# Turning a recurrence's outputs into matmul features by VectorE block transposes and a trip through DRAM

## The chip, the cores and the metric

One core of a Trainium2 chip runs the program. The metric is the device time of one execution in microseconds (us). Before the change three runs gave 671.13, 673.59 and 679.51 us; the median is 673.59. The profile is one further execution, taken by the hardware profiler.

A core has five engines with a queue each, run in order: PE (TensorE, the matmuls), DVE (VectorE), ACT (ScalarE), POOL (GpSimd) and SP (SyncE, which here issues nearly all DMAs). They wait for one another by semaphores. Matmul results land in PSUM, from which DVE or ACT carry them to SBUF.

## The reference

The inputs are q, k and v (4 x 8 x 768 x 48: batch, head, token, width) and beta (4 x 8 x 768). Two blocks follow each other:

```python
k_n = k / (np.linalg.norm(k, axis=-1, keepdims=True) + 1e-06)
for t in range(S):                               # a recurrence per (batch, head)
    y[:, :, t] = q_t @ state
    v_old = k_t @ state
    state = state + b_t * outer(k_t, v_t - v_old)
x = y.transpose(0, 2, 1, 3).reshape(3072, 384)   # 4*768 tokens, 8 heads x 48
h = x @ w_in                                     # 384 -> 2048
out = (h * np.cos(h)) @ w_out                    # 2048 -> 384
```

## The kernel before

**Units and pairs.** The 768 tokens are cut into 24 units of 32 tokens. A unit n holds 32 tokens of all 4 batches and 8 heads; the partitions are 4 batches x 32 tokens. Inside a unit the recurrence becomes matrices: `gram(n)` (PE) multiplies keys with keys and queries; a triangular matrix per head is inverted column by column, for a pair of units at once, by POOL (`inverse`, lines L656 and L663; the first pair by DVE). The way to the inverse leads through DRAM: `gram_put` writes g_dr, `gram_get` reads it as gb, `put` writes z_dr, `get(n)` reads zt. Then per unit, on PE: `state(n)` (keys and queries times the state, into the PSUM tile p_kq), `solve(n)` (p_u, from zt and the right side rhs), `update(n)` (p_s, the state's increment), `within(n)` (adds the part from inside the unit to p_kq). DVE carries out what lies between (`right`, `solve_out`, `update_out`, which changes the state st that `state(n+1)` reads).

**Outputs to features.** After `within(n)` the outputs y lie in p_kq with tokens on partitions. The second block needs features on partitions. So `within_out(n)` (L825, ACT) copies p_kq to the SBUF tile y, `features(n)` (L829, PE) transposes y in three 128 x 128 steps into the PSUM tile p_z (which shares the single bank "two" with p_g, p_u and p_s), and `features_out(n)` (L839, ACT) copies p_z into one half of x_ffn, which holds the features of a pair p of units (2p and 2p+1).

**The second block** runs on pairs. For pairs 0 and 1 `hidden` (L856) multiplies x_ffn with w_in directly. From pair 2 on `x_sum(p)` (L927, DVE) forms differences of the features, one in place, and `layer(p, s, i)` (L975) uses a scheme of sums that needs fewer products. ACT and DVE compute h cos(h): `turns`, `rest`, `cos`, `gate`. `output` (L1001, pair 0) or `product` (L1058) multiply by w_out; `collect` sums; SP stores.

**Weights** arrive as 64-bit words: `weights` (SP), `split` (ACT), `shift` (DVE), `add` (POOL), 28 pieces in the first part of the run.

**The order.** The class `Order` keeps a list of tasks. Every task has a key, an engine, tiles that it makes and uses, and what it depends on. `LINE` is a list of 1,879 numbers written out in the file: the order in which the tasks' instructions are emitted. `run` (L157) follows it, and every engine's queue is pinned to it. So the sequence on each engine is fixed by LINE, and the costs given to `add` do not act at run time. Tiles rotate through few buffers: one p_kq, one "two", one y, two zt, two x_ffn.

## Time and profile before

| what | value |
|---|---|
| three runs | 671.13, 673.59, 679.51 us |
| span of the profiled execution | 670.2 us |
| DVE busy, whole span | 466.5 us, 70% |
| ACT | 242.4 us, 36% |
| POOL | 347.1 us, 52% |
| p_z transposes (L835) on PE | 72 of them, 273 ns median, 12.2 us busy |
| y copies (L827) and x_ffn copies (L843) on ACT | 24 each, 478 ns median |
| DVE transposes kq_t<-qp (L531), 128x1024 | 16, 1,236 ns median |
| DVE transpose t_beta<-bq (L376), 128x768 | 1, 968 ns |
| SP's DMA queue | 212,516 packets, 49.16 MB |

The span is the time from the first to the last recorded event of the core; the measured time of a run lies a little above it. "Busy" is the time in which an instruction of that engine was running; matmuls overlap, so their single durations add up to more than the time that they take from PE. "SPq" is the queue of SP, whose rows are the issue of DMAs and not the moving of the data. A row such as "L835 PE MATMUL p_z<-consts,y x3" names line, engine, operation, the tile written and the tiles read, and the count. In a list of waits a row has the waiting engine and group, the engine and group that released it, and then the us in total, the times, and the longest.

### The profile page before, as it was taken

Reading aid. Unit: us, or ns where it says so; the run is one execution under the profiler, and the core shown is the slowest. Engines: PE = TensorE matmul, PEld = TensorE weight load, DVE = VectorE, ACT = ScalarE, POOL = GpSimd, SP = SyncE. Lnnn points to the kernel's source line nnn. Section 1 sums busy time; section 2 is a strip of 40 time slices with the busy share of each in tenths; the row PEclk is TensorE's granted clock in tenths of the full one; section 3 lists DMA queues with packets and bytes.
Section 4 is the critical chain, followed back from the end, with each engine's and each line's share of the span. In section 5 each row is a group of like instructions: output and inputs, shape, how many; then the busy total and the mean of one; then the engine's idle time right before and its main releaser. Section 6 shows DMA issues by size and latency. Waiting matters only on the chain.

```text
span 670.2 us, 27723 instructions
## 1 busy us (share of the span) xinstructions
PE 616.5 (92%) x12120; PEld 580.5 (87%) x12120; DVE 466.5 (70%) x892; ACT 242.4 (36%) x416; POOL 347.1 (52%) x734
## 2 busy tenths in 40 slices
PE   4326789999999999999999999999999999999996
PEld 3225779976889999999999999999999999999996
DVE  6872698897577777787767767777776666656662
ACT  3441565650223433334334332333323333332420
POOL 4268778988728658238458484385383382000000
PEclk9999899999899999999999999999999999999999
DMA  8776594464364523544443624623312302000000
GB/s 179 183 177 156 130 228 124 105 110 66 53 103 68 85 54 57 89 88 70 70 83 55 108 35 73 106 39 53 69 27 39 68 2 40 20 2 24 1 25 24
DMA packets 215645, 51.80 MB, mean 77 GB/s; under 512 B 207076, under 2 KB 210420, under 8 KB 215524
## 3 DMA queue, kind: packets, MB, share of 16 engines
q1 hardware_dynamic: 212516, 49.16, 38.0%
q8 instruction: 95, 1.56, 1.0%
q10 hardware_dynamic: 2752, 0.43, 0.4%
q0 software_dynamic: 256, 0.44, 0.2%
q14 instruction: 26, 0.21, 0.1%
HBM read 39.24 MB, written 10.75 MB: 75 GB/s over the span
## 4 chain that ended last, share of the span: by engine, by line
PE 79%; DMA 7%; SPq 4%; POOL 4%; DVE 2%; issue 2%; ACT 0%; ACTq 0%; DVEq 0%; POOLq 0%
PE p_h L975 28%; PE p_out L1058 27%; PE p_h L856 5%; PE p_kq L713 4%; PE p_out L1001 3%; PE p_u L776 3%; PE p_s L799 3%; PE p_kq L816 2%; PE p_g L546 2%; POOL z L663 2%; DMA pairs<-in_moe_w_in_dram 2%; POOL part L656 2%; PE p_o L1058 2%; DMA qp<-in_q_dram 1%; SPq L310 1%
## 5 line engine op out<-in xcount | busy, mean ns | idle before, releaser
L656 POOL TENSOR_TENSOR part<-z,gb 128x126 f32<-128x126 f32 (+22 forms) x341 | 134.6, 395 | 116.1 <-DMA gb<-g_dr 75.0
L663 POOL TENSOR_TENSOR z<-z,part 128x126 f32<-128x126 f32 (+22 forms) x341 | 138.7, 407 | 26.7
L975 PE MATMUL p_h<-x_ffn,w_in 128*128 128x128 f32 x1120 | 143.0, 277 | 0.0
L975 PEld LDWEIGHTS p_h<-x_ffn,w_in 128*128 128x128 f32 x1120 | 134.2, 192 | 1.5
L1058 PE MATMUL p_out<-w_out,g_ffn 128*128 128x192 f32 x672 | 121.8, 330 | 2.0 <-issue 2.0
L1058 PEld LDWEIGHTS p_out<-w_out,g_ffn 128*128 128x128 f32 x672 | 108.7, 191 | 3.3 <-issue 2.1
L896 ACT ACTIVATE turns<-p_h,quarter_turn 128x512 int32<-128x512 f32 x96 | 65.8, 688 | 105.6 <-DVE p_h L994 72.1
L912 ACT ACTIVATE turns<-turns,halfpi 128x512 f32<-128x512 f32 x96 | 68.7, 721 | 64.3 <-DVE turns L903 63.7
L1058 PE MATMUL p_out<-w_sum,g_ffn 128*128 128x192 f32 x496 | 88.7, 329 | 0.0
L903 DVE SCALAR_TENSOR_TENSOR turns<-p_h,turns 128x512 f32<-128x512 f32 x96 | 65.3, 683 | 22.0 <-ACT turns L896 22.0
L1058 PEld LDWEIGHTS p_out<-w_sum,g_ffn 128*128 128x128 f32 x496 | 79.7, 190 | 0.8
L991 ACT COPY g_ffn<-p_h 128x512 f32<-128x512 f32 x60 | 35.0, 584 | 108.8 <-PE p_h L975 108.7
L1074 DVE TENSOR_TENSOR g_ffn<-g_ffn 128x512 f32<-128x512 f32 x88 | 62.3, 715 | 10.0 <-PE p_out L1058 8.9
L915 DVE TENSOR_TENSOR g_ffn<-turns,p_h 128x512 f32<-128x512 f32 x96 | 64.6, 677 | 6.6 <-ACT turns L912 6.5
L994 DVE TENSOR_TENSOR p_h<-g_ffn,p_h 128x512 f32<-128x512 f32 x60 | 41.5, 692 | 30.5 <-PE p_h L975 23.7
L467 POOL TENSOR_TENSOR knrm<-ksum,halves 128x16 f32<-128x16 f32 (+1 forms) x14 | 36.2, 2590 | 41.5 <-DVE ksum L455 41.5
L1108 DVE SCALAR_TENSOR_TENSOR o<-p_out,o 128x192 f32<-128x192 f32 x74 | 25.2, 353 | 35.4 <-PE p_out L1058 33.9
L856 PE MATMUL p_h<-x_ffn,w_in 128*128 128x128 f32 x384 | 47.3, 282 | 2.3 <-POOL part L656 2.1
L856 PEld LDWEIGHTS p_h<-x_ffn,w_in 128*128 128x128 f32 x384 | 45.8, 197 | 3.3 <-issue 2.2
L975 PE MATMUL p_h<-x_sum,in_sum 128*128 128x128 f32 x320 | 41.6, 277 | 0.0
L786 DVE TENSOR_TENSOR u<-p_u,bz 128x384 f32<-128x384 f32 x48 | 24.4, 550 | 21.9 <-PE p_u L776 21.8
L975 PEld LDWEIGHTS p_h<-x_sum,in_sum 128*128 128x128 f32 x320 | 38.7, 192 | 0.5
(110 smaller groups left out, 767.2 us busy)
## 6 DMA issues: line engine op xcount, KB each, us to landing
pairs<-in_moe_w_in_dram SPq DMA_DIRECT2D x12, 512.0 KB
pairs<-in_moe_w_out_dram SPq DMA_DIRECT2D x16, 384.0 KB
gb<-g_dr SPq DMA_DIRECT2D x22, 256.0 KB
vp<-in_v_dram SPq DMA_DIRECT2D x96, 48.0 KB
out_dram<-o SPq DMA_DIRECT2D x23, 192.0 KB
kp<-in_k_dram SPq DMA_DIRECT2D x128, 24.0 KB
z_dr<-z SPq DMA_DIRECT2D x11, 256.0 KB
zt<-z_dr SPq DMA_DIRECT2D x88, 32.0 KB
```

The source lines that it names most:

```text
L467: nc.gpsimd.tensor_tensor(out=scales[m][2][:, part], in0=sums[m, part.start][:, 0:n], in1=halves[:, 0:n], op=ALU.pow,)
L656: eng.tensor_tensor(out=part, in0=z[:, 0:rows, j, None].to_broadcast(shape), in1=a[:, j, None, j + 1 :].to_broadcast(shape), op=ALU.mult,)
L663: eng.tensor_tensor(out=behind, in0=behind, in1=part, op=ALU.subtract)
L856: nc.tensor.matmul(p_h[:, i], w_in[:, t, (4 * k + i) * 128 : (4 * k + i + 1) * 128], xts[p][:, t, unit * 128 : (unit + 1) * 128], start=(t ...
L896: nc.scalar.activation(turns[p, f], hidden_of(p, f), AF.Identity, bias=quarter_turn, scale=TURN)
L903: nc.vector.scalar_tensor_tensor(out=r, in0=hidden_of(p, f), scalar=TURN, in1=t, op0=ALU.mult, op1=ALU.subtract,)
L912: nc.scalar.activation(r, r, AF.Sin, bias=halfpi, scale=2.0 * math.pi)
L915: nc.vector.tensor_tensor(out=place(p, f), in0=step_of(rests.pop((p, f)), f), in1=step_of(hidden_of(p, f), f), op=ALU.mult,)
L975: nc.tensor.matmul(p_h[:, e], in_sum[:, odd_tile, 4 * s + e] if a == "s" else w_in[:, a, f * 128 : (f + 1) * 128], x_sums[p][:, unit] if b ...
L994: nc.vector.tensor_tensor(out=block(p, s, 0, 1) if i == 3 else p_h, in0=block(p, s, *one), in1=p_h, op=ALU.add,)
L1058: nc.tensor.matmul(p_o, left(p, part, a)[:, e % 4], right(e, b), start=(e == 0), stop=(e == FT // 2 - 1), skip_group_check=True,)
L1074: nc.vector.tensor_tensor(out=left(p, s, to), in0=left(p, s, one), in1=left(p, s, two), op=op)
```

## The change

For units 4 and later (`MOVED = 4`) the three steps from p_kq to x_ffn are replaced:

- `within_turn(n)` on DVE: one stream transpose of the 384 output columns of p_kq into the SBUF tile y. It turns each block of 32 tokens x 32 features in its place, so that y has 32 features on the 32 partitions of a batch.
- `within_put(n)` on SP: four DMAs, one a batch, write y to a DRAM tile y_dr laid out as 128 features x 4 batches x (3 x 32): pieces of 96 numbers, 384 bytes.
- `features_move(n)` on SP: one DMA reads y_dr into the half of x_ffn, 128 partitions of 384 numbers.

x_ffn changes its layout for all units, from [128, 3, 256] to [128, 2, 4, 3, 32]: unit, batch, feature block, token. What reads it (`hidden`, `layer`, `x_sum`) takes four runs of 32 columns in place of one run of 128. Units 0 to 3 keep the transposes on PE.

`LINE` is another order of the tasks throughout, from the first loads to the last unit. Two tasks at the start (the load of beta and its spreading) now also account for the buffers that they hold.

```diff
@@ constants
+    MOVED = 4
@@ after features(n)
     def features_out(n):
         if n % 2 == 0:
-            xts[n // 2] = ffn_pool.tile([128, KT, TOK], FP, name="x_ffn")
-        cols = slice((n % 2) * 128, (n % 2 + 1) * 128)
-        nc.scalar.copy(xts[n // 2][:, :, cols], p_zs.pop(n))
+            xts[n // 2] = ffn_pool.tile([128, 2, B, KT, C], FP, name="x_ffn")
+        nc.scalar.copy(
+            xts[n // 2][:, n % 2].rearrange("p b k t -> p k b t"),
+            p_zs.pop(n).rearrange("p k (b t) -> p k b t", t=C),
+        )
+
+    def moved(p, t, unit):
+        return xts[p][:, unit, :, t]
+
+    def within_turn(n):
+        y = ys[n] = work.tile([128, KT * 4, C], FP, name="y", bufs=1)
+        nc.vector.transpose(
+            y.rearrange("p (z k) t -> p k z t", k=KT),
+            p_kqs.pop(n)[:, :, 1].rearrange("p a j e -> p j a e"),
+        )
+
+    def within_put(n):
+        y = ys[n]
+        ys[n] = dram.tile([128, B, KT * C], FP, name="y_dr")
+        dst = ys[n].rearrange("(z i) b c -> b i z c", i=C)
+        for b in range(B):
+            nc.sync.dma_start(
+                out=dst[b], in_=y[quarter(b)].rearrange("i (z k) t -> i z (k t)", k=KT)
+            )
+
+    def features_move(n):
+        if n % 2 == 0:
+            xts[n // 2] = ffn_pool.tile([128, 2, B, KT, C], FP, name="x_ffn")
+        nc.sync.dma_start(
+            out=xts[n // 2][:, n % 2].rearrange("p b k t -> p b (k t)"), in_=ys.pop(n)
+        )
@@ hidden, layer: the moving operand
-                    xts[p][:, t, unit * 128 : (unit + 1) * 128],
+                    moved(p, t, unit),
@@ x_sum
-        t = x_sums[p] = ffn_pool.tile([128, 3, 128], FP, name="x_sum", bufs=1)
-        u0, u1 = slice(0, 128), slice(128, 256)
+        t = x_sums[p] = ffn_pool.tile([128, 3, B, C], FP, name="x_sum", bufs=1)
         for to, one, two in (
-            (t[:, 1], xt[:, 1, u1], xt[:, 0, u1]),
-            (xt[:, 0, u1], xt[:, 0, u1], xt[:, 0, u0]),
...
+            (t[:, 1], moved(p, 1, 1), moved(p, 0, 1)),
+            (moved(p, 0, 1), moved(p, 0, 1), moved(p, 0, 0)),
...
@@ the tasks of a unit, after within(n)
+        if n >= MOVED:
+            add(("within_turn", n), "DVE", 0.5, lambda: within_turn(n), [("within", n)],
+                makes=[("y", ("y", n))], uses=[("p_kq", n)])
+            add(("within_put", n), "SP", 0.45, lambda: within_put(n), [("within_turn", n)],
+                makes=[("y_dr", ("y_dr", n))], uses=[("y", n)], moves=1.0)
+            add(("features_out", n), "SP", 1.8, lambda: features_move(n),
+                [("within_put", n)] + ([("features_out", n - 1)] if second else []),
+                makes=[] if second else [("x", ("x", m))], uses=[("y_dr", n)], moves=1.0)
+            return
```

Around units 4 and 5 the two orders stand as follows on PE (keys of tasks; the number in parentheses is the unit, or pair and step):

```
before: solve(4) out(1,0,0) update(4) within(4) out(1,0,1) features(4) state(5) out(1,1,0) solve(5) out(1,1,1)
        update(5) within(5) out(1,2,0) features(5) out(1,2,1) layer(2,0,0)
after:  solve(4) out(0,1,0..3) update(4) within(4) out(1,0,0) state(5) out(1,0,1) solve(5) out(1,1,0) out(1,1,1)
        update(5) within(5) out(1,2,0) out(1,2,1) gram(8) state(6) gram(9) out(1,3,0) out(1,3,1) layer(2,0,0)
```

## The prediction

> **What bounds the kernel now.** I read the page's busy shares and slices first. The third row is PE (TensorE) by fortieths of the span.

> ```profile
> PE 616.5 (92%) x12120; PEld 580.5 (87%) x12120; DVE 466.5 (70%) x892; ACT 242.4 (36%) x416; POOL 347.1 (52%) x734
> ...
> PE   4326789999999999999999999999999999999996
> ```

> PE is open only in the first six slices (100 us); after that it is full. The windows view puts numbers on stages (PE busy, then PEld, DVE, ACT, POOL, granted clock, DMA share, GB/s):

> ```profile
> 0.00:102.00 102.00, 58.31 (x1568) 50.62 (x1569) 71.08 (x164) 43.82 (x80) 65.06 (x102) 0.98 0.76 174
> ...
> 166.00:212.00 46.00, 42.48 (x987) 39.69 (x985) 28.66 (x55) 12.24 (x20) 27.20 (x66) 0.96 0.44 71
> 212.00:430.00 218.00, 218.00 (x4506) 209.38 (x4495) 163.20 (x309) 79.68 (x134) 125.09 (x287) 1.00 0.44 74
> ```

> From 212 to 430 us PE has no gap. The waits of PE alone, from 102 us on, agree:

> ```profile
> PE p_u L776 <- DMA zt<-z_dr: 2.6, 2, 1.6
> PE p_out L1058 <- issue: 2.0, 1, 2.0
> PE p_h L856 <- issue: 0.3, 1, 0.3
> ```

> So past 102 us whatever leaves PE's queue shortens the run by its slot there. The slot is read in the timeline of PE (start, busy, line):

> ```profile
> 407.17 0.49 PE L835 MATMUL p_z<-consts,y 128*128 128x128 f32 x3
> 407.50 1.06 PE L975 MATMUL p_h<-x_ffn,in_sum 128*128 128x128 f32 x8
> ```

> The three transposes show 0.49 us, but the next group starts 0.33 us after them; matmuls overlap.

> **Part 1, PE.** Units 4 to 23 lose their three transposes: 20 x 0.33 = 6.6 us. By the rows, going from a 32-row group back to a 128-row group costs about 0.2 us (a p_out group of 8 takes 1.50 after a small group, 1.30 else). Counted in the two orders from the third solve on, there are 73 such returns before and 71 after: 0.4 us. Sum on PE: -7.0 us. The moving operand x_ffn now comes in four runs of 32 columns. The gram matmul already moves two runs of 32 (0.65 us for 64 of them, 64 columns each) beside a state matmul with 48 columns in one run (1.31 us for 128): the same 10 ns each. I take nothing; a rate halved by the runs would add 142 us (1280 matmuls with x_ffn moving x 0.111), and this row speaks against it.

> **Part 2, ACT and DVE.** ACT loses 40 copies of 0.478 us (19.1 us); it is 36% busy, so nothing is gained. DVE gets 20 transposes of 384 columns. The two transpose rows give 1.236 us for 1024 columns and 0.968 us for 768, which by their slope is 0.56 us for 384; 0.97 bounds it above, the 0.26 us of the 192-column copy below. 20 x 0.56 = 11.2 us. From 212 to 430 us that is ten units, 5.6 us on 163 busy of 218: 77%, hidden by DVE's own gaps. On DVE's queue the transpose of unit 5 stands ahead of its update_out, and each holds p_kq, so state(n+1) on PE waits for it. PE's cover between within(n) and state(n+1) is at least 0.9 us (unit 14), 1.3 us (units 4 and 16), more elsewhere; turn plus its release (0.7 us) fits unless DVE is mid-instruction, so I take 0.5 us in all and keep 0 to 2.

> **Part 3, the trip.** Each unit adds four puts and one move on SP. SP's rows show 1.97 us for four zt issues and 1.13 for two gb issues, so 2.0 + 0.55 us. A landing is read here:

> ```profile
> 195.53 3.70 DMA zt<-z_dr
> 199.22 0.14 issue
> 199.36 1.36 PE p_u L776 x64
> ```

> This is the chain of waits. SP's rows have eight zt issues in 4.05 us from 195.53 on, so the first four were issued by 197.5 and had landed at 199.2: 1.7 us. At 427.88 the same took 2.0 us after its last issue. z_dr writes landed 3.2 and 5.1 us after theirs, as writes of 128 and 256 KB in small pieces. Trip: turn 0.56 + puts 2.0 + landing 2.0 + move 0.55 + landing 2.0 = 7.1 us; with the z_dr rows for the put, 8.3 to 10.2. Cover, as PE time by rows in the new order from within(n) to the first layer step that reads the unit: 16.6 us (unit 4) to 36 for even units, and for odd ones 10.5 us (unit 5), 14.3 (unit 7), 14.8 to 24 beyond, of which x_sum takes 1.3. Only unit 5 is near. So the trip's length is hidden, at 0 to 1 us. If the cover went, one late pair would cost its excess and then a slow start: after the 1.95 us gap at 166 us the next rows took 2.03 for 7 matmuls, 1.44 and 1.69 where 1.14, 0.73 and 1.50 are usual, 1.8 us more.

> [...]

> **Part 4, SP.** 20 x 2.55 = 51 us of issues, and the move waits on SP for its puts to land with little between them in some units (none for 15, 18, 20; a store of 0.6 us for 5, 9, 11, 17): some 10 us more up to unit 17. SP is in order, so zt, gb and k loads stand behind that. Adding issue times by rows, SP's total goes from 342 to 393 us in 662; but between 212 and 430 us, where nearly half the units fall, SP idles some 45 us now and gets 10 x 2.55 + 5 = 31. The new order defers k, v and block loads: get(6) stands 8.8 us earlier in SP's sum, get(8) 0.7 us earlier, while their solves stand 2.4 and 5.8 us earlier in PE's. Now get(6) ended 64 us beyond SP's sum (197.5 to 133) and solve(8) began 72.5 beyond PE's (243.0 to 170.5). With these and 3.5 us of move waits, get(8) lands at 163.5 + 64 + 3.5 + 2 = 233 us; solve(8) is due at 164.7 + 72.5 less some 5 of gains = 232. The same for solve(10) leaves 5 us, and more later. I take 1 us of stall, range 0 to 6.

> **Part 5, the new order at the start.** Before 102 us PE waits 43.5 us, some 12 of them after 46 us. Up to the third solve the new order has two more hidden groups ahead (2 x 2.68) and one output group behind it (2.68): 2.7 us more work in those gaps. POOL's second inverse may start 3 us sooner (two weight adds and the norms are rearranged) but holds five adds inside instead of three (2 x 1.27). I take -2.7 us, range -8 to +3. Then solve(4) stands 10.4 us earlier on PE; its inverse loses two norms of 2.9 us ahead of it on POOL, so it is ready at about 147 us against a wish of 146: 1.2 us of stall and 1.1 of slow start, +2.3, range 0 to 6. The stall of solve(6) (1.57 and 0.6 of slow start) and that at 433 us (1.0 + 0.4) were late loads behind SP, whose margins grow: -2.5 of 3.6.

> Sum: -7.0 + 0.5 + 0.5 + 1 - 2.7 + 2.3 - 2.5 = -7.9 us, a span of 662.3 us. The lowest of the three runs is 0.9 us above the profiled span of 670.2, the median (673.6) 3.4 above. I put 2.2 on it, between the two: **664.5 us**, 9.1 below the median.

> **Rivals.**
> (a) *The gain is given back.* Unit 5's trip, solve(4), solve(8) and state(15) each stall at the top of their ranges: 1 + 6 + 6 + 2 against 4.3 taken, 11 us more: 675 us. For it: the tight margins just named. Against: only two stalls of more than 1 us stand after 102 us now.
> (b) *SP becomes the bound: slower.* If a put lands after 5.1 us (z_dr at 83 us) instead of 2.0, the move holds SP 3.1 us longer in each of 20 units. In the twelve units up to 430 us that is 37 us on top of 31, beyond the 45 free by 23; zt loads slip by it and PE stalls, 23 + a few slow starts of 1.8: 662.3 + 28 + 2.2 = 692 us. It decides from a landing of about 4 us on. For it: both writes to DRAM that the trace times take over 3 us. Against: those are 128 KB and 256 KB of 128-byte pieces with weights loading (DMA share 0.76), in the middle the share is 0.44. [...] The g_dr writes here, of 128-byte pieces, held SP's gets only 3.2 us in six waits, which speaks against (b).
> (c) *The order, not the transposes, carries it.* If the start gains 8 us and the later stalls vanish, -7.0 - 8 - 3.6 + 1 = -17.6: 655 us. For it: 12 us of waits lie open. Against: POOL's chain (inverse of pair 1, ending at 83 us) limits how soon solve(2) can go.
> (d) *The transposes stay on PE.* The built order shows only those of units 0 to 3: no chance.

> **Chances.** Forecast (658 to 670) 0.53, (c) 0.20, (a) 0.17, (b) 0.10. The range leaves out the far half of (c) and (b): 655 to 680. A difference of 2%, about what a measurement can tell from none, is 660.1 or less and 687.1 or more against 673.6. Faster by it: (c) and a fringe of the forecast, 0.25. Slower: (b), 0.10. Within: 0.65.

> **What would show it.** No p_z rows after unit 3, PE's slot sum 7 us less; a stream transpose from p_kq at 0.5 to 0.65 us; y_dr landing in 2 to 3 us; PE waits on x_ffn's move or x_sum below 1 us; solve(2) no later than 92 us. Wrong: PE waits past 102 us above 8 us in sum, with zt or y_dr as releaser and SP without gaps between 166 and 430 us; or matmuls with x_ffn moving slower than 0.111 us.

## The result, and the profile after

The changed kernel takes 695.01 us (median of 694.17, 690.64, 701.65 and 695.85); the kernel before took 674.32 us beside it (four runs). The ratio is 1.0324, with a 95% interval of 1.0258 to 1.039: slower. One of the four runs, 701.65, is over 1.5% above the fastest and is left out of the ratio. The profiled span is 692.4 us against 670.2, so 22.2 us more where the prediction had 7.9 less.

The page of the changed kernel, busy shares and slices (PE by fortieths of the span, then its granted clock):

```profile
PE 616.5 (89%) x12060; PEld 578.0 (83%) x12060; DVE 470.8 (68%) x912; ACT 224.7 (32%) x376; POOL 348.0 (50%) x734
...
PE   4236869999899889999999899899898999999997
...
PEclk9555999999999999999999999999999999999999
```

The 60 transposes are gone (12,060 matmuls for 12,120), but PE's row is no longer a row of nines: there are eights up to slice 31 of 40 (some 535 us). The windows view of the changed kernel (PE busy first, then PEld, DVE, ACT, POOL, clock, DMA share, GB/s):

```profile
0.00:102.00 102.00, 53.73 (x1464) 46.80 (x1465) 61.00 (x150) 40.42 (x75) 62.09 (x94) 0.73 0.68 155
...
212.00:430.00 218.00, 207.60 (x4385) 197.25 (x4384) 160.47 (x306) 70.19 (x111) 126.31 (x286) 0.99 0.48 87
430.00:665.00 235.00, 227.90 (x3829) 220.49 (x3828) 152.72 (x284) 70.72 (x115) 80.70 (x195) 0.98 0.26 53
```

From 212 to 430 us PE had no gap before; now 10.4 us are open. (The clock of 0.73 in the first stage, 0.98 before, differs between executions: over the whole span the four of the changed kernel had 0.95, 0.95, 0.98 and 0.98. It is taken up under the start below.) What PE waits for past 102 us (total, times, longest):

```profile
PE p_kq L712 <- issue: 7.8, 5, 2.1
PE p_g L545 <- issue: 4.9, 2, 2.7
PE p_out L1082 <- DVE g_ffn L942: 3.0, 2, 2.0
PE p_out L1082 <- ACT o L1119: 2.3, 1, 2.3
PE p_kq L712 <- DVE y L851: 1.3, 1, 1.3
PE p_u L775 <- DMA zt<-z_dr: 0.9, 3, 0.4
```

All waits past 102 us come to 22.4 us (4.9 before), and 13.9 of them are "issue" (2.3 before): PE stands still and the profile knows nothing that it waits for. One of these in the timeline of PE (start, duration, what, and in brackets the idle time ahead of it):

```profile
487.05 0.85 PE L545 MATMUL p_g<-kq_t 48*32 48x64 f32 x63
...
487.75 1.35 PE L712 MATMUL p_kq<-st,kq_t 48*32 48x48 f32 x124
491.18 0.28 PE L712 MATMUL p_kq<-st,kq_t 48*32 48x48 f32 x1 [2.08 <-issue]
491.39 3.45 PE L1000 MATMUL p_h<-x_ffn,w_in 128*128 128x128 f32 x16
```

state(18) runs through 127 of its 128 matmuls, stops for 2.08 us, issues the last one, and then the 16 matmuls of a layer step take 3.45 us instead of the usual 1.8. The windows view of that place shows why the step is slow, a granted clock of 0.50 for 3.42 us:

```profile
490.94:494.36 3.42, 3.18 (x15) 3.10 (x16) 1.16 (x2) 0.00 (x0) 0.00 (x0) 0.50 0.48 77
```

To place the loss, I assigned every matmul record to its task and subtracted a standard slot for each kind of task (the slot that it has in undisturbed stretches of the kernel before; the sum is 576.7 us before and 569.9 after). What is left is PE's lag. After minus before it is +3.8 us at 102 us, +3.3 at 212, +18.0 at 430, +28.4 at 560 and +29.1 at the end; with the 6.8 us of work saved that is the 22.4 us by which the last matmul ends later. By cause: issue gaps +11.6, other waits past 102 us +5.9, half clock +4.5 (four such stretches past 102 us cost 5.6, the one before 1.1), start +3.8; the remaining 3.3 us are small and not assigned.

### The profile page after: what moved, and what is told of

Read it like the earlier page. It is cut to its first block, busy times and chain, and to the rows that moved or that the text cites. A ratio compares the mean times of both kernels' runs of the same rounds, so it can differ in the third digit from the quotient of the medians.

```text
span 692.4 us, 27712 instructions
## 1 busy us (share of the span) xinstructions
PE 616.5 (89%) x12060; PEld 578.0 (83%) x12060; DVE 470.8 (68%) x912; ACT 224.7 (32%) x376; POOL 348.0 (50%) x734
## 3 DMA queue, kind: packets, MB, share of 16 engines
q10 hardware_dynamic: 2752, 0.43, 0.4%
## 4 chain that ended last, share of the span: by engine, by line
PE 76%; DVE 5%; SPq 5%; POOL 5%; issue 4%; DMA 4%; ACT 0%; DVEq 0%; ACTq 0%; POOLq 0%
PE p_h L1000 27%; PE p_out L1082 26%; PE p_h L883 7%; PE p_kq L712 4%; PE p_u L775 3%; PE p_s L798 3%; PE p_kq L815 2%; PE p_g L545 2%; SPq L309 2%; SPq L320 2%; DMA qp<-in_q_dram 2%; PE p_o L1082 2%; POOL knrm L466 1%; POOL part L655 1%; PE p_out L1025 1%
## 5 line engine op out<-in xcount | busy, mean ns | idle before, releaser
L662 POOL TENSOR_TENSOR z<-z,part 128x126 f32<-128x126 f32 (+22 forms) x341 | 142.5, 418 | 26.7
L1000 PE MATMUL p_h<-x_ffn,w_in 128*128 128x128 f32 x1120 | 147.5, 280 | 0.0
L1000 PEld LDWEIGHTS p_h<-x_ffn,w_in 128*128 128x128 f32 x1120 | 138.9, 196 | 1.5 <-DVE g_ffn L942 0.2
L1082 PE MATMUL p_out<-w_sum,g_ffn 128*128 128x192 f32 x496 | 90.5, 330 | 0.0
L942 DVE TENSOR_TENSOR g_ffn<-turns,p_h 128x512 f32<-128x512 f32 x96 | 64.6, 679 | 11.8 <-ACT turns L939 10.7
L883 PE MATMUL p_h<-x_ffn,w_in 128*128 128x128 f32 x384 | 49.4, 290 | 2.0 <-DVE g_ffn L942 0.7
L883 PEld LDWEIGHTS p_h<-x_ffn,w_in 128*128 128x128 f32 x384 | 47.5, 205 | 3.5 <-DVE g_ffn L942 1.3
L1018 DVE TENSOR_TENSOR p_h<-g_ffn,p_h 128x512 f32<-128x512 f32 x60 | 41.3, 689 | 13.2 <-PE p_h L1000 11.4
L712 PE MATMUL p_kq<-st,kq_t 48*32 48x48 f32 x2944 | 33.9, 214 | 12.7 <-issue 11.3
L712 PEld LDWEIGHTS p_kq<-st,kq_t 48*32 48x32 f32 x2944 | 29.9, 105 | 15.8 <-issue 13.3
```

The source lines that it names most:

```text
L662: eng.tensor_tensor(out=behind, in0=behind, in1=part, op=ALU.subtract)
L712: nc.tensor.matmul(p_kq[quarter(b), par, a, j], kq_t[rows48(par), a, b * NP + j], st[rows48(par), b // 2, j, b % 2], start=(j == 0 and a = ...
L883: nc.tensor.matmul(p_h[:, i], w_in[:, t, (4 * k + i) * 128 : (4 * k + i + 1) * 128], moved(p, t, unit), start=(t == 0), stop=(t == KT - 1),)
L942: nc.vector.tensor_tensor(out=place(p, f), in0=step_of(rests.pop((p, f)), f), in1=step_of(hidden_of(p, f), f), op=ALU.mult,)
L1000: nc.tensor.matmul(p_h[:, e], in_sum[:, odd_tile, 4 * s + e] if a == "s" else w_in[:, a, f * 128 : (f + 1) * 128], x_sums[p][:, unit] if b ...
L1082: nc.tensor.matmul(p_o, left(p, part, a)[:, e % 4], right(e, b), start=(e == 0), stop=(e == FT // 2 - 1), skip_group_check=True,)
```

## Experiments

Theory after the comparison: the new order (O) or the new path (P) brings the stalls.

**Each half alone.** The first kernel has the new path in the old `LINE`, the second the new `LINE` with all units on the old path:

```diff
@@ e1_path_old_order, to the changed kernel: the list of the kernel before
-0 1 2 3 4 5 6 1767 10 72 14 37 11 15 42 38 73 12 7 1771 39 16 40 43 44 13 17 45 19 46 18 96 48 79 20
+0 1767 1 2 14 10 11 12 3 7 4 37 5 42 15 72 6 38 13 39 16 43 73 40 1768 1771 17 44 19 96 75 1769 97
...
@@ e2_order_old_path
-    MOVED = 4
+    MOVED = NU
```

> The changed kernel with the order of the kernel before (each unit's three new steps in the places of the three old ones, one for one), so the new path without the new order. Theory O (the order costs the time: it starts later and lays groups of small matmuls side by side, and the PE waits there for its own instructions): some 660 to 672 us; PE idle named issue after 102 us stays near the 2.3 us of before, hidden(0,10) begins near 102 us. Theory P (the path costs it: the two DMA trips a unit, 0.4 MB more in DRAM traffic, delay the PE's instruction fetches or arrive late): 685 to 700 us, with 10 us or more of issue gaps, or of waits on x_ffn or zt, in the old order too. A middle result with waits of layers on x_ffn (the old order gives features 2 us, not 7) would say that the path needs some new order.

Measured: 734.33 us, ratio 1.0918 (1.0865 to 1.0971), above the ranges of both theories. hidden(0,10) begins at 102.9 us, as O wants. But the old order gives the trip too little room, as the waits of PE past 102 us show:

```profile
PE p_h L1000 <- DVE x_sum L962: 13.2, 4, 7.0
PE p_kq L712 <- issue: 6.7, 4, 3.2
...
PE p_h L1000 <- DMA x_ffn<-y_dr: 4.8, 1, 4.8
```

> The changed kernel with no unit moved (TensorE transposes for all 24 units, no y_dr), in the new order; each unit's transposes and their copy stand at the first place behind the turn's place where the PSUM bank that they need is free. Theory O: 695 to 703 us (the new order's losses and the transposes' 7 us besides), issue gaps of 10 us or more after 102 us, hidden(0,10) near 109 us. Theory P: 672 to 682 us, issue gaps near 2.3 us.

Measured: 694.73 us, ratio 1.0352 (1.0293 to 1.041): with no trip at all the new order is as slow as the changed kernel. Its issue gaps come to 9.6 us; another 4.4 us are waits of the transposes for their bank, which come from the places that they have in this order. hidden(0,10) begins at 106.6 us. Order and path are both dear, and O does not say why gaps without a cause appear in either (10.2 us in the old order with the path).

**Where the gaps lie.** Counting PE's matmuls from the program's start, every issue gap past 102 us lies at nearly the same place modulo 128: in the changed kernel the gaps of 2.70, 1.92, 1.69, 1.83, 2.08 and 2.21 us stand ahead of matmuls 3133, 4153, 4534, 7084, 9123 and 10014, which are 61, 57, 54, 44, 35 and 30 modulo 128 (the place creeps by 4 to 5 in 1,000). The waits for other engines of 1.0 us and more stand at 52, 92, 36 and 100. 128 matmuls with their weight loads are 256 instructions, and one of the page's instruction queues (packets, MB, share) moved 95 pieces of 16,384 bytes for 24,120 loads and matmuls, which comes to 64.5 bytes each and 254 to a piece:

```profile
q8 instruction: 95, 1.56, 1.0%
```

Each of these gaps begins while such a piece is being fetched (0.9 to 1.6 us), and PE goes on 1.3 to 1.6 us after it has ended. When PE goes on with matmuls 3133, 7084 and 10014, this queue has brought 24, 55 and 78 pieces, and the pairs issued until then fill 24.5, 55.3 and 78.2: one piece for each that was used up. So theory F: PE waits for its own program, which comes in blocks, one a piece, reckoned here at 128 pairs. A gram and a state side by side are 192 pairs in 1.9 us; when a block edge falls into the first 64 pairs, a second one follows inside the run, and the block between was used up faster than the next came.

**Moving the program under the edges.** gram(0), or half of it, is issued twice, at 11 us, where PE waits for inputs. Nothing else changes, except that all later instructions stand 64 (or 32) pairs later:

```diff
@@ gram (f1_before_shift64 and f2_after_shift64; 2 in place of 4 for the shifts of 32)
-        for j in range(NP):
+        for j in [*range(NP)] + [i % NP for i in range(4 if n == 0 else 0)]:
```

> The kernel before, with the 64 load-and-matmul pairs of gram(0) issued twice (0.65 us of PE work at 11 us, where the PE waits for inputs). Theory F (the issue gaps are the PE waiting for its own program, which comes in blocks of 16 KB = 128 pairs; a gram and state side by side, 192 pairs in 1.9 us, run dry when they begin in the wrong part of a block): the shift moves the eight gram+state runs from places 36 to 106 of a block, where they do not stall, to places 100 to 128 and 0 to 42, so 5 to 7 stalls of 2 to 3 us, some with half a clock behind them: 682 to 694 us. Rival O (the new order's stalls come from its waits and from what stands beside the groups, not from where the groups lie in the program) and rival T (from the added DMA traffic): under 1 us, 672 to 675 us.

Measured: 707.77 us, ratio 1.0523 (1.046 to 1.0585). 0.65 us of matmuls in an idle place cost the kernel before 35 us. PE now stops in ten of its states, by 1.4 to 2.8 us:

```profile
PE p_kq L713 <- issue: 20.5, 10, 2.8
```

First the timeline of the kernel before at gram(18) and state(16), then the same place in the shifted kernel:

```profile
413.44 1.36 PE L713 MATMUL p_kq<-st,kq_t 48*32 48x48 f32 x127
414.73 2.87 PE L1058 MATMUL p_out<-w_out,g_ffn 128*128 128x192 f32 x16
```

```profile
443.15 1.16 PE L713 MATMUL p_kq<-st,kq_t 48*32 48x48 f32 x104
447.09 0.54 PE L713 MATMUL p_kq<-st,kq_t 48*32 48x48 f32 x23 [2.78 <-issue]
447.56 5.40 PE L1058 MATMUL p_out<-w_out,g_ffn 128*128 128x192 f32 x16
```

The same matmuls, a stop of 2.78 us in their middle, and then the product at half speed. This settles F against O and T: the order is the old one, and the trip's DMAs are not in this kernel at all. The time is 14 us above the range of F; part of that is the start, where hidden(0,10) begins at 110.2 us instead of 102.2.

> The changed kernel with the same 64 pairs more at 11 us. Theory F: the stalls move: gram(11)-state(8), gram(17)-state(14) and gram(21)-state(18) lose theirs, gram(13)-state(10), gram(15)-state(12) and gram(19)-state(16) get one each of 2 to 3 us; the two runs of 256 pairs (units 6 and 20) stall as before; the time stays within 4 us of the changed kernel's 695. Rivals O and T: the stalls stay where they were.

Measured: 697.64 us (ratio 1.0356, 1.031 to 1.0403), and the stalls moved as expected: gram(11), gram(17) and gram(21) lost theirs; gram(13), (15) and (19) have 1.9, 2.7 and 2.5 us. Three more came that were not expected, of 1.8, 2.4 and 1.4 us at 119, 148 and 416 us; issue gaps come to 18.1 us in all.

> The changed kernel with 32 pairs more at 11 us. Theory F: gram(11)-state(8) and gram(17)-state(14) come to places 36 and 44 and lose their stalls (4.4 us and what half clock follows), gram(21)-state(18) goes to place 4 and keeps it; 685 to 692 us. Rivals O and T: 695 us, the same stalls.

Measured: 700.98 us (1.0422, 1.0388 to 1.0456), a miss. The runs of gram(11) and gram(17) keep 1.1 and 1.8 us, since their first edge (57 and 44) still lies 21 and 0 pairs behind their start; and a wait for g_ffn grew to 5.2 us.

> The changed kernel with the order changed so that no gram stands beside a state on the PE: one group of large matmuls (0.9 to 1.3 us, 8 pairs) between them. Theory F: the stalls of 1.9 to 3 us at units 6, 8, 14, 18 and 20 go, with the half clock behind two of them: 678 to 684 us; issue gaps after 102 us under 4 us. Rivals O and T: 692 to 698 us.

```diff
@@ order on PE in g1_after_split (tasks; the other runs of gram and state in the same way)
-out(2,1,0) gram(11) state(8) layer(3,0,0)
+gram(11) out(2,1,0) state(8) layer(3,0,0)
```

Measured: 691.63 us (1.028, 1.0247 to 1.0312), 3.4 us less and not 11 to 17. The stalls of units 8 and 14 fell to 0.3 and 0.4 us, but PE still stops for 1.6 us in gram(9), 2.0 in state(9) and 1.3 in state(18), and gram(9) then waits 0.9 us for a bank that is now late. Issue gaps are 7.0 us, where under 4 was expected. So it is not neighbours alone that matter, but how long a whole block takes. The following rule was fitted to all traces so far: PE waits for the rest when less than 3.6 us pass between the time it stands 24 pairs ahead of a block's first pair and the time it reaches the block's end. Over the standard slots this gives 0.1 us of stalls for the kernel before, 11.5 for the changed one, and between 3.8 and 23.6 for the kernel before under any other shift in steps of 16 pairs (16 pairs: 5.1). By this reckoning the kernel before stood in the only quiet place, and the changed kernel's 11.5 us lie within what the old order has at other places. Of these shifts only 64 and 32 were run.

> The kernel before with 32 pairs more at 11 us (half of gram(0) issued twice, 0.33 us). Theory F, now with a size: a block of 128 pairs must take 3.6 us from 24 pairs ahead of its first one, or the PE waits for the rest; over the nominal durations of the groups that makes 0.1 us of stalls for the kernel before, 23.6 with the shift of 64 (measured: about 24, and 10 of half clock), 11.5 for the changed kernel, and 11.8 us in 4 long stalls for this one: with half clock 684 to 692 us. Rival: 672 to 675 us.

Measured: 688.42 us (1.0208, 1.0178 to 1.0239), inside the range that this reckoning gave ahead, and with the four long stalls that it named (2.0 to 2.3 us); issue gaps are 13.2 us in all.

**Aligning the changed kernel.**

```diff
@@ h1_after_aligned, gram; and in LINE gram(8) two large groups later, gram(11) two earlier, gram(17) two later
-        for j in range(NP):
+        for j in [*range(NP)] + [i % NP for i in range({20: 2, 17: 2}.get(n, 0))]:
```

> The changed kernel with three groups moved (gram(8) two large groups later, gram(11) two earlier, gram(17) two later, with what hangs on them) and with 32 pairs of gram(17) and of gram(20) issued twice (0.33 us each): by the same reckoning 2.7 us of stalls are left of 11.5, all of them in units 16 and 20. Theory F: 680 to 686 us; a residue over the 664 of the forecast that is waits on DVE, ACT and DMA and the later start. If stalls come from something else: 692 us or more.

Measured: 695.92 us (1.034, 1.0323 to 1.0358). Not a microsecond gained, a miss by 10 us. The stalls in units 6, 8, 14 and 18 are gone, and issue gaps fell from 13.9 to 5.6 us; yet the other waits of PE past 102 us rose from 8.5 to 15.8 us. Two of the rows:

```profile
PE p_out L1082 <- DVE g_ffn L942: 7.9, 2, 4.0
PE p_kq L712 <- issue: 3.4, 3, 1.7
```

Behind the first of them, DVE's timeline, and SP's at the same place:

```profile
237.20 0.29 DVE L962 TENSOR_TENSOR x_sum<-x_ffn 128x128 f32<-128x128 f32 x1 [3.82 <-DMA x_ffn<-y_dr]
```

```profile
230.69 0.61 SPq L597 DMA_DIRECT2D g_dr<-g  x1
231.35 3.34 SPq L309 DMA_DIRECT2D vp<-in_v_dram  x4
234.73 0.45 SPq L868 DMA_DIRECT2D x_ffn<-y_dr  x1
```

g_ffn is late because x_sum stands ahead of it on DVE; x_sum waits for the move, which lands 2.0 us after its issue but stood on SP behind g_dr writes and v loads. The stalls at block edges had partly hidden that SP was late.

> The same, with the order of the kernel before up to features_out(3) and the new order for what is left. If the new order at the start costs the 4 us by which the changed kernel lags at 102 us: 3 to 5 us less than the run with the new start, 676 to 682 us; hidden(0,10) begins within 1 us of 102.2 us. If the start is covered by later slack: the same time as that run.

Measured: 688.23 us (1.02, 1.016 to 1.024), 7.7 us less than with the new start. In the profiled executions hidden(0,10) begins at 101.8 us for 107.5, 5.7 us sooner, and the spans differ by the same 5.7 us (686.4 for 692.1): what the start gains is kept to the end. The time is above the range given, since SP's lateness stayed. The half clock at the start is not what makes the new start late: the changed kernel's execution, at 0.73 over the first 102 us, begins hidden(0,10) at 105.9 us, and the aligned kernel's, at 0.95, at 107.5.

> The changed kernel with the 100 DMA starts of the trip (four puts and one move a unit) issued by the ACT engine instead of SP. If SP's fuller queue (82% busy with issues from 212 to 430 us, 71% before) makes blocks and stores late, which the PE then waits for behind g_ffn and o (2.0 us at 327 us, 2.25 us at 440 us, 1.0 at 235 us): 688 to 692 us and those waits gone. If SP is not late: 693 to 698 us. If ACT, which now waits for within_turn and spends 2.3 us a unit on issues, holds up turns and cos: over 698 us.

```diff
@@ h3_after_trip_on_act: within_put and features_move
-            nc.sync.dma_start(
+            nc.scalar.dma_start(
```

Measured: 709.21 us (1.0526, 1.0497 to 1.0554). ACT's queue now holds the trip's 100 starts among its own work; PE waits 6.0 us in one piece for g_ffn, and its issue gaps grew to 17.2 us. This run can't say what SP costs.

> The changed kernel with the same plain trip and nothing else changed (the PE's program is the same, so the stalls at block edges stay where they are, 11.5 us by the reckoning; again the permutation over token groups is left out). SP theory: the waits on g_ffn at 327 us (2.0 us) and on o at 440 us (2.25 us), with the half clock behind them (1.4 and 1.3 us), go: 687 to 691 us. If these waits are not SP's: 693 to 697 us.

```diff
@@ h6_after_plain_trip (and h5_aligned_plain_trip, on the aligned kernel): within_put
-        ys[n] = dram.tile([128, B, KT * C], FP, name="y_dr")
-        dst = ys[n].rearrange("(z i) b c -> b i z c", i=C)
-        for b in range(B):
-            nc.sync.dma_start(
-                out=dst[b], in_=y[quarter(b)].rearrange("i (z k) t -> i z (k t)", k=KT)
-            )
+        ys[n] = dram.tile([128, 4, KT * C], FP, name="y_dr")
+        nc.sync.dma_start(out=ys[n].rearrange("p z c -> p (z c)"), in_=y.rearrange("p z t -> p (z t)"))
@@ features_move
-            out=xts[n // 2][:, n % 2].rearrange("p b k t -> p b (k t)"), in_=ys.pop(n)
+            out=xts[n // 2][:, n % 2].rearrange("p b k t -> p b (k t)"),
+            in_=ys.pop(n).rearrange("p z c -> p (z c)"),
```

These kernels do not compute the reference: without the permutation the features stand in other places. They time the trip alone.

Measured: 688.25 us (1.021, 1.0162 to 1.0257), 6.8 us less than the changed kernel; the wait for o is gone, that for g_ffn is 0.9 us.

> The run with the old start and the aligned program, with the trip as one put and one move of whole rows (2 DMA starts a unit for 5, the same bytes); it leaves the permutation over token groups out, so x_ffn holds the features in another place. If what is left over the forecast is SP's queue (60 starts of 0.45 us less, 27 us): the waits of x_sum on x_ffn at 225 us (4.2 us) and of g_ffn behind blocks at 325 us (3.3 us) shrink below 1 us each, 676 to 682 us. If it is the trip's latency or the position of x_sum in the order: 686 to 689 us.

Measured: 675.78 us (ratio 1.000, 0.9962 to 1.0039), 12.4 us less than the same kernel with five starts, 0.2 us below the range of the SP theory. With five starts the longest waits of PE past 102 us were for g_ffn, one of them behind an x_sum that waits 4.0 us for the move:

```profile
PE p_out L1082 <- DVE g_ffn L942: 7.5, 2, 4.2
```

With two starts that one is gone, and 1.2 us of the other are left:

```profile
PE p_kq L712 <- issue: 3.5, 3, 1.4
PE p_u L775 <- DMA zt<-z_dr: 1.7, 4, 0.9
PE p_g L545 <- DVE tt L579: 1.3, 2, 0.9
PE p_out L1079 <- DVE g_ffn L939: 1.2, 1, 1.2
```

The plain trip also writes larger pieces, so one run keeps them and has five starts again:

```diff
@@ h8_plain_four_puts, to h5_aligned_plain_trip
-        nc.sync.dma_start(out=ys[n].rearrange("p z c -> p (z c)"), in_=y.rearrange("p z t -> p (z t)"))
+        for b in range(B):
+            nc.sync.dma_start(
+                out=ys[n][quarter(b)].rearrange("p z c -> p (z c)"),
+                in_=y[quarter(b)].rearrange("p z t -> p (z t)"),
+            )
```

> The run with the plain trip, old start and aligned program (675.8 us), but with four puts a unit again, one a batch, each of 32 whole rows: as many DMA starts on SP as in the changed kernel, the pieces as large as in the plain trip (the permutation over token groups is left out here too). If the plain trip gained its 12 us by SP's fewer starts: 684 to 689 us, near the 688.2 of the run with the real trip. If by the larger pieces of the writes (1,536 bytes for 384): 675 to 679 us.

Measured: 686.76 us (1.021, 1.0153 to 1.0268), and the waits are back:

```profile
PE p_out L1083 <- DVE g_ffn L943: 5.4, 2, 3.2
```

It is the number of starts on SP, not the size of the pieces. SP's issues take 383 us in sum with two starts a unit, and 415 and 419 us with five (small and large pieces). Three starts less also make each trip itself about 1.3 us shorter (0.43 us each); no run separates that from the shorter queue.

So three things together cost the changed kernel its gain: block edges, SP's queue, and the start. With most of them out (675.8 us, with the permutation left out) it is level with the kernel before (674.7 beside it). The 6.8 us of PE work saved are mostly eaten by small waits of the kind above: PE's waits past 102 us are 10.3 us there, 4.9 in the kernel before. How the loss divides is known in part. The plain trip alone gains 6.8 us; the aligned program and the old start gain another 12.5 us with it, of which the start is 5.7 to 7.7 by the runs above. The aligned program alone gained nothing, and with the plain trip it was not run alone. No kernel that computes the whole reference beat the kernel before; a trip with two starts that also permutes was not tried.

## Why the prediction was wrong

- **PE, -7.0: the size was right, its use was wrong.** The p_z rows end after unit 3, the slots saved come to 6.8 us, and a matmul with x_ffn moving in four runs takes 275 ns in the median, as before. The step that failed is "past 102 us whatever leaves PE's queue shortens the run by its slot there". It takes PE's remaining groups at fixed slots, but three pairs less a unit, and a new order, also move nearly the whole of PE's program against its block edges, and that was worth 11.6 us of gaps and two of the four stretches at half clock (the other two follow waits for g_ffn and o). The prediction itself showed the hint, `p_out <- issue: 2.0`, a gap ahead of matmul 2752 (64 modulo 128), and read it as nothing that could grow. (Its bound of 142 us for a halved rate leaves out the 384 matmuls of hidden, whose x_ffn comes in four runs too; with them it is 185 us.)
- **DVE, +0.5 (0 to 2): within its range.** A turn takes 0.576 us (0.56 said), and the one wait of state behind y is 1.3 us.
- **The trip, +0.5: its legs were right, its cover was not.** Unit 5's puts ended on SP at 184.3 us and the move was issued at 185.9, so they landed in 1.6 us; the move lands in 2.0 (issued by 235.2 us and landed at 237.2 in the aligned kernel). But the cover was reckoned from within(n) as if SP were free for the trip. x_sum waited 5.1 us for it in the changed kernel (two waits), and 3.8 us at once when the stalls no longer hid it.
- **SP, +1 (0 to 6): mis-sized.** The trip's issues were sized rightly (some 49 us of SP's time, 51 said), their cost was not: with three starts less a unit the changed kernel gains 6.8 us, the aligned one 12.4. Setting 31 us of issues against 45 us of idle time counted SP's idle time as one pool. On SP's queue a late start held up those behind it: in the aligned kernel the move of 234.73 us stood behind 6 us of g_dr writes and v loads. It reached PE by way of DVE (x_sum, then g_ffn) and ACT (o), while the prediction looked for zt, whose waits fell to 0.9 us.
- **The start, -2.7 (-8 to +3): wrong sign.** It lags 3.8 us at 102 us, and the old start gave back 5.7 us by the profiles and 7.7 by the runs. Weighing the PE work laid into gaps missed that PE there waits for q and k loads; these waits grew from 14.8 to 20.9 us. The stall of solve(4), +2.3, did not come; the old stall of solve(6) went, as said.
- **Rivals.** (b) named 692 us, close to 695, and SP indeed became late, but by its starts and not by slow landings of the puts (1.6 us, where it needed 4), and only as one of three causes. (a) and (c) did not happen; no rival had the block edges. Of the signs named for being wrong, the one that asks for PE waits with zt or y_dr as releaser would have missed the 13.9 of 22.4 us that have no releaser.

## What to carry to other kernels

Where PE runs many small matmuls, look for "issue" gaps at places that repeat about every 128 load-and-matmul pairs (127.4 in the changed kernel): an order that was good in one place of the program lost 5% here when 64 pairs were added far ahead of it, so compare two versions only after each has been tried under a few shifts. Keep large matmuls between runs of small ones, so that no 128 pairs take less than about 3.6 us by the reckoning above; one large group between gram and state was not enough here (3.4 us gained). Count added DMA starts against the in-order queue that issues them and against what stands behind each start, not against that queue's idle time: three starts less a unit gained 6.8 and 12.4 us here.
